# One read of 4608 bytes a row for q and k, and one for v, from the third pair of heads on

## The chip, the cores and the metric

The kernel runs on one core of one Trainium2 chip. The metric is device time in microseconds (us) of one launch. Before the change three runs took 440.33, 440.87 and 443.41 us; the median is 440.87. One more execution was taken with the profiler on: it took 437.04 us, of which 435.3 us lie between the first and the last profiled instruction (the span).

## The reference

Inputs are q, k and v of 8 batches, 8 heads, 576 positions and 64 channels in fp32, a forget gate f, and three weights. Decay attention comes first, then a gated MLP with a causal convolution of five taps:

```python
scores = scale * np.matmul(q, k.transpose(0, 1, 3, 2))
cum = np.cumsum(np.log(np.clip(f, 0.0001, 1.0)), axis=-1)
decay = cum[:, :, :, None] - cum[:, :, None, :]
scores = np.where(causal, -1000000000.0, scores + decay)
attn = softmax(scores)                      # rows, with 1e-9 in the sum
x = np.matmul(attn, v)                      # heads side by side: 512 channels
gate_pre += conv_w[k] * xp[:, k:k + S, :]   # summed over 5 taps
out = (1 / (1 + np.exp(-gate_pre))) * (x @ w_val) @ w_out
```

## The kernel before

Heads are taken two at a time: one head on partitions 0 to 63, the other on 64 to 127. That gives 32 pairs, four to a batch. The letters below are used throughout.

- **Loads.** `load_pair(i)` reads q and k of pair i into one of three buffers `Xr` (128 rows of 1152 fp32): two reads of 576 elements (2304 bytes) a row, q and then k. `load_rest(i)` reads v of the pair into one of three buffers `vt`: a read of 640 elements and one of 512.
- **S**, the scores (`plan_s`): small matmuls on 64x64 tiles give q times k plus the decay, in three groups of PSUM banks. VectorE (DVE) finds each row's maximum (line 421, written to `negm`), ScalarE (ACT) takes the exponential into `P` (line 425).
- **T and U** (`plan_pt`): DVE turns the 32x32 blocks of `P` into `T` (line 460), two copies fill half of `U` (line 250, on ACT, DVE or GpSimd, which is POOL in the rows), and four DMAs of `T` fill the other half from other partitions.
- **PV** (`plan_pv`): 108 matmuls on 64x64 tiles of `U` with `vt`, then three DVE steps (line 517) that multiply by the row sums' inverses (`zb`, which goes through DRAM as `zd`) and give `x`. Of `x`, `xh` and `xl` are the high and the low part.
- **Mv and Mo** (`plan_moe`): per batch the two products with the weights, each as three matmuls of high and low parts on the full 128x128 array. They are the bulk of TensorE's (PE's) work from the first batch on.
- **Start.** The gate f is clipped, its logarithm is summed (scan), and `split` cuts the sums into three bf16 parts that are placed in `st_70`: three casts with two DVE steps between them (line 347). The S matmuls of pair 1 and later read `st_70`. Both weights are decoded by DVE, ACT and POOL beside the first pairs (lines 693 to 709, tiles `sl`, `sh`, `ot`, `wall`), and pairs 0 and 1 take the convolution on PE (**CV**).

No scheduler runs: the string `ORDER` holds, packed, one list of all steps in the order of issue, the engine of each step that has a choice, and the PSUM bank of each product. Every engine, and the queue of SP that starts nearly all DMAs, works through its part of that list in order. A DMA on SP waits for the one eight places ahead of it to land, besides the semaphores of its data. Lines 235, 250 and 262 are helpers that record matmuls, copies and DMAs, so these rows are told apart by their tiles.

Of the kernel before, what the change touches and what calls it, by code (L numbers as in the profile page):

```python
# [41 lines left out]
NF = 16  # L42
PART = ((0, 32, 48), (0, 16, 32))
ORDER = (
    "c-l>pc}!G!w#Vz<y0!0n)vf*3erw<N?beRI1kjfN`bSgpk_Pz$kVzDsL`o-7WD=mA1ZZB;(EcIlB!G4T=p+s8OB&=Qio8USKN@rrK_>y^4?$k?prmKstyKNaId#tGd(Q"
# [3 lines left out]
    "4h=EQAQbLy(Xo;3DxEagA_|{s!nEbP-AfkQ^jaz)fJ3be-~o@{za;>;qTHT(FnWMH!<EQYtBvq&kWO9Hu-aE)!2v_-u%Tkq?P`L^^4L(n~3kU*Yhe21G$OxJ8+v)Kd!N"
    "CdvV2meNgL1uMWL*h*;v?-Qm76ND;omas|zs5_K(%3JUZnN3PjQ>4?(^W-$;A(_r@CO43W$nE4b^DeoAvOuW^TftxH{d9x`lTebAbQKgc&Vf{_gt|eWr0>!Z#t0o_R8U"  # L50
    "=vP5M54lnyeM=+pE$dXQ0Im>AWJ?+G8ld*riJ3S))NqlQUoyq4;r=1Jq^8qy9}MY2#i_!;sXd4YU~u}&_5Fn)=A0B(}i_-~k8#vAhglAD;dj1FcGbB5W+_(TRNt<2w;T"
    "g*=8EOUohPim${sOPEeR4R+Zx=b~)8>nlXF6IGqf!Rf+QOtNA<qinoC6t#;fHlY*W76;?Y9AG2PcR3l!^|@*7aL|3*dx@>)Jj@C<35{B3(#EnpQvHHhO)$-W3Mu6XkuC"
    ";euX_sE#QOfBCU>v&=Rz6dPIPuH8X}7cj?y{^Xwt~GN&5<ka3gI&Zxz=;b*8d><jo=>J|JXyN%t)o@NiQe`Zi=MRqm&3cHc5;@-e_;lIN_WvE%_nfDlv8B2^3`z*78Wn"
    "wKbDrg(*Vf<xUT0j>;qIT94EzP>kZf1E{5!N-<Y1VbxbLuJs<!*Cc(8ll+`2V5)Ok2Rerma%{PJM!ZiJ!$EaO${JF2EgOzrk<dx2Qd|ewvBG;hJb$_?xVc92vWw>*O}l"
    "D!5f#7cImcp>@&L8A<LfRts0lJ}sb2cBq4_OSBPIA8VAh&)8vX&=zPN+%9g7pqJap{lJ!T5Y8vIh4Wf)$mVk(37zwf198%vqF|6qVGeUQX%Wt8&Li3f#wQxgZ4``gHv}"
    "HeXIg+Rrh~#J?prRN`GmD8pa@4<w*+m1E$*CPkBg&I>63z8!H7UbPtd2i6WnF)6~Vs1MDG*GnQL5?h)-YSKI8J32=l*K3oMlBW=;zR1eKh5!KmPr@D=L~3*w=oN)cbg="
# [36 lines left out]


# [698 lines left out]
```

## Time and profile before

| quantity | value |
|---|---|
| median of three runs | 440.87 us |
| profiled execution | 437.04 us, span 435.3 us |
| PE matmul busy | 416.7 us (96%) |
| DVE busy | 373.7 us (86%) |
| ACT busy | 338.1 us (78%) |
| POOL busy | 287.9 us (66%) |
| DMA traffic of the SP queue | 85.28 MB in 74328 packets, 71.1% of 16 engines |

Busy shares are means over stages that differ. The reader should look at which engine is full in which stage, and what TensorE waits for where it is not full. Idle time of an engine that nothing waits for costs nothing.

### The profile page before, as it was taken

The numbers are of one execution on the slowest core, as the hardware profiler recorded it, in microseconds if no ns is written. First come the engines' busy times: TensorE is split into PE (matmuls) and PEld (weight loads), VectorE is DVE, ScalarE is ACT, GpSimd is POOL, SyncE is SP. The second block draws the span as 40 slices with busy tenths as digits, with TensorE's granted clock in tenths as the row PEclk, the third lists the DMA queues.
The fourth block names the chain that finished last, engine by engine and source line by source line (L and its number), as shares of the span: only waits on it lengthen the run. The fifth ranks groups of instructions, "written<-read, shape, count | busy, mean of one in ns | idle before, by whom it ended". The sixth has DMA issues, their size and how long they took to land.

```text
span 435.3 us, 16742 instructions
## 1 busy us (share of the span) xinstructions
PE 416.7 (96%) x6660; PEld 356.1 (82%) x6660; DVE 373.7 (86%) x1034; ACT 338.1 (78%) x840; POOL 287.9 (66%) x295
## 2 busy tenths in 40 slices
PE   7679899999999989999999999999999999999996
PEld 5456678888998878888898889887898888988885
DVE  6999889998999888898899987978999987997751
ACT  7899879998888869888777877667987988763430
POOL 4575847587959692898779475898675779752200
PEclk9899999999999999999999999999999999999999
DMA  7889987878777975977885677777867776387112
GB/s 286 291 213 240 239 233 196 223 206 210 216 202 199 253 199 152 256 211 200 220 249 143 184 212 206 197 209 216 243 174 209 223 184 191 74 205 224 57 46 98
DMA packets 74694, 86.93 MB, mean 200 GB/s; under 512 B 48120, under 2 KB 48120, under 8 KB 74616
## 3 DMA queue, kind: packets, MB, share of 16 engines
q1 hardware_dynamic: 74328, 85.28, 71.1%
q8 instruction: 52, 0.85, 0.8%
q10 hardware_dynamic: 288, 0.59, 0.4%
q14 instruction: 26, 0.21, 0.2%
HBM read 51.99 MB, written 10.26 MB: 143 GB/s over the span
## 4 chain that ended last, share of the span: by engine, by line
PE 88%; DVE 4%; DMA 3%; ACT 2%; issue 1%; POOL 1%; SPq 0%; POOLq 0%
PE banks L235 88%; DVE banks L421 2%; DMA U<-T 1%; DMA vt<-in_v_dram 1%; DVE T L460 1%; ACT P L425 1%; DMA cwu<-in_conv_w_dram 1%; POOL wall L709 1%; DVE negm L421 0%; ACT L334 0%; SPq L262 0%; POOL U L250 0%; DVE sh L707 0%; ACT sl L693 0%; ACT gate L333 0%
## 5 line engine op out<-in xcount | busy, mean ns | idle before, releaser
L425 ACT ACTIVATE P<-banks,negm 128x576 f32<-128x576 f32 (+8 forms) x288 | 150.0, 530 | 42.4 <-DVE negm L421 30.7
L421 DVE CUSTOM_DVE_ANT_0 banks<-banks,mk 128x576 f32<-128x576 f32 (+8 forms) x288 | 135.3, 508 | 15.2 <-PE banks L235 11.4
L562 POOL TENSOR_TENSOR gate<-gate,tm 128x576 f32<-128x576 f32 x77 | 109.7, 1425 | 33.6 <-DVE gate L560 12.0
L460 DVE STREAM_TRANSPOSE T<-P 128x1088 f32<-128x1088 f32 (+2 forms) x96 | 110.5, 1165 | 5.2 <-ACT P L425 2.8
L235 PE MATMUL banks<-xh,wall 128*128 128x288 f32 x512 | 107.1, 298 | 0.0
L235 PE MATMUL banks<-Xr 64*64 64x288 f32 (+8 forms) x1280 | 103.1, 410 | 1.4 <-DMA Xr<-in_x_dram 1.4
L235 PEld LDWEIGHTS banks<-U,vt 64*64 64x64 f32 x3456 | 91.8, 135 | 8.3 <-issue 3.1
L235 PE MATMUL banks<-U,vt 64*64 64x128 f32 (+1 forms) x3456 | 93.2, 256 | 3.8 <-issue 1.8
L235 PE MATMUL banks<-wall,hh 128*128 128x512 f32 x288 | 90.4, 395 | 0.0
L235 PEld LDWEIGHTS banks<-xh,wall 128*128 128x128 f32 x512 | 83.3, 188 | 4.2 <-issue 1.4
L235 PEld LDWEIGHTS banks<-Xr 64*64 64x64 f32 x1280 | 63.8, 134 | 16.5 <-issue 5.9
L235 PE MATMUL banks<-xl,wall 128*128 128x288 f32 x256 | 75.4, 295 | 0.0
L235 PEld LDWEIGHTS banks<-wall,hh 128*128 128x128 f32 x288 | 52.6, 188 | 13.0 <-issue 1.6
L425 ACT ACTIVATION_READ_ACCUMULATOR P<-banks,negm 128x1 f32 x288 | 58.7, 204 | 0.0
L250 ACT COPY U<-T 128x1440 f32<-128x1440 f32 x40 | 55.5, 1396 | 3.4 <-DVE T L460 1.7
L235 PE MATMUL banks<-wall,hl 128*128 128x512 f32 x144 | 56.2, 390 | 0.0
L235 PE MATMUL banks<-st,pk 64*64 64x448 bf16 (+8 forms) x620 | 45.8, 291 | 7.5 <-ACT st L250 3.7
L257 POOL TENSOR_SCALAR tm<-x,cw 128x576 f32<-128x576 f32 x40 | 30.1, 753 | 34.1 <-DVE gate L560 13.3
L235 PEld LDWEIGHTS banks<-xl,wall 128*128 128x128 f32 x256 | 48.0, 188 | 0.3
L607 POOL TENSOR_TENSOR hl<-h,hh 128x576 fp32r<-128x576 f32 (+2 forms) x34 | 34.4, 1027 | 12.6 <-DVE gate L560 4.1
L526 POOL TENSOR_TENSOR xl<-x,xh 128x576 fp32r<-128x576 f32 x25 | 35.6, 1430 | 10.6 <-DVE sl L695 4.9
L235 PEld LDWEIGHTS <-pk 64*64 64x64 bf16 x620 | 25.6, 106 | 20.0 <-issue 16.2
(104 smaller groups left out, 482.8 us busy)
## 6 DMA issues: line engine op xcount, KB each, us to landing
U<-T SPq DMA_DIRECT2D x128, 180.0 KB
Xr<-in_x_dram SPq DMA_DIRECT2D x63, 288.0 KB
vt<-in_v_dram SPq DMA_DIRECT2D x32, 320.0 KB
out_dram<-ot SPq DMA_DIRECT2D x36, 256.0 KB
vt<-in_v_dram SPq DMA_DIRECT2D x32, 256.0 KB
zb<-zd SPq DMA_DIRECT2D x64, 80.0 KB
zb<-zd SPq DMA_DIRECT2D x64, 64.0 KB
sl<-in_w_out_dram SPq DMA_DIRECT2D x2, 512.0 KB
```

What stands on the lines that cost most here:

```text
L235: nc.tensor.matmul(out, lhsT=lhsT, rhs=rhs, start=start, stop=stop)
L250: (eng.copy if eng is nc.scalar else eng.tensor_copy)(out=out, in_=in_)
L257: eng.tensor_scalar(out=out, in0=in_, scalar1=col, scalar2=0.0, op0=ALU.mult, op1=ALU.add)
L421: nc.vector.tensor_tensor_reduce(out=sl, in0=sl, in1=mk[:, S - ext:], op0=ALU.add, op1=ALU.min, scale=-0.125, scalar=3.0e38, accum_out=neg ...
L425: nc.scalar.activation(out=dst, in_=bank(key)[:, a0:a0 + ext], func=AF.Exp, bias=negm[r][:, col], scale=-1.0, accum_out=zs[r][:, col])
L460: nc.vector.transpose(out=bass.AP(Tt.tensor, Tt.offset + 32 * FB[js[0]], [pitch, (32, nk), (CW, 2), (1, 32)]), in_=Pt[u])
L526: any_("xl", {"POOL": 1.4, "DVE": 0.67}, p, lambda eng: eng.tensor_tensor(out=xl[s], in0=xv, in1=xh[s][:, :].bitcast(F32), op=ALU.subtract ...
L562: eng.tensor_tensor(out=gt, in0=gt, in1=to, op=ALU.add)
L607: eng.tensor_tensor(out=hl[jj][:, y:y + x1 - x0], in0=h2[jj % 2][:, x0:x1], in1=hh[jj][:, y:y + x1 - x0].bitcast(F32), op=ALU.subtract)
L709: any_(nm, {"POOL": 1.2, "DVE": DM / 960.0 + 0.075}, p, lambda eng, lo=lo, zz=zz, m=m: eng.tensor_tensor(out=lo, in0=zz, in1=m, op=ALU.mul ...
```

## The change

From pair 2 on `load_pair` issues one DMA for the whole row of q and k (1152 elements, 4608 bytes) and `load_rest` one for the whole row of v. Pairs 0 and 1 keep two reads each. Consumers are the same: S of a pair waited for both halves of `Xr` before, and PV for both parts of `vt`. The list in `ORDER` is another one, for all engines.

```diff
 ORDER = (
-    "c-l>pc}G!G!w#Vz<y0!0n)vf*3erw<N?beRI1kjfN`bSgpk_Pz$kVzDsL`o-7WD=mA1ZZB;(EcIlB!G4T=p+s8OB&=Qio8USKN@rrK_>y^4?$k?prmKstyKNaId#tGd(Q"
+    "c-l>pdrTC2mdCrQtKaYHclEpaUHyJ{SHG(t2(k$ve*n74h3g-JYy#*cf^Kp_C%JH$1dvI9>n4J3BIqW7P6Ay2xS*3<kWCPsM9@tx=p=$nBFH9!OtR4So!RPi|IRsm&gX"
...
     def load_pair(i):
         r = i % XB
+        if i > 1:
+            load("load", 1.62, i - 1.0, Xr[r], x[i], (), [("Xr", r, n) for n in range(2)])
+            return
         for n in range(2):
             c = slice(S * n, S * n + S)
             load("load", 0.81, i - (1.0 if i else 9.0) + 0.02 * n, Xr[r][:, c], x[i][:, c], (), [("Xr", r, n)], early=i == 0)
 
     def load_rest(i):
         r = i % 3
+        if i > 1:
+            load("load", 1.5, i - 0.2, vt[r], v[i], (), [("vt", r, n) for n in range(2)])
+            return
         for n, c in enumerate((slice(0, 5), slice(5, NJ))):
             load("load", 0.75, i - (0.2 if i else 7.0) + 0.02 * n, vt[r][:, c], v[i][:, c], (), [("vt", r, n)])
```

Sixty DMAs go: 30 of `Xr` and 30 of `vt`. SP starts 406 instead of 465, since one read of pair 0 that ACT started is now also started by SP. Line numbers of the changed kernel are 5 higher behind the loads and 1 lower ahead of them.

The order of VectorE near the start, from the first of the two steps that cut the summed logarithms (`gate` is their buffer, `st_70` the bf16 table) to the first turns of pair 0. Before:

```order
L347 SCALAR_TENSOR_TENSOR gate<-st_70,sel,gate 128x576
L421 ISA banks,negm_90<-banks,mk 128x64
L421 ISA negm_90 128x1
L250 CAST st_70<-gate 128x576
L421 ISA banks,negm_90<-banks,mk 128x128
L421 ISA negm_90 128x1
L347 SCALAR_TENSOR_TENSOR gate<-st_70,sel,gate 128x576
L421 ISA banks,negm_90<-banks,mk 128x384
L421 ISA negm_90 128x1
L460 STREAM_TRANSPOSE T_83<-P_81 128x16x2x32
```

The same place on VectorE with the change:

```order
L352 SCALAR_TENSOR_TENSOR gate<-st_70,sel,gate 128x576
L426 ISA banks,negm_90<-banks,mk 128x256
L426 ISA negm_90 128x1
L426 ISA banks,negm_90<-banks,mk 128x128
L426 ISA negm_90 128x1
L706 TENSOR_SCALAR sh<-sh 128x512
L352 SCALAR_TENSOR_TENSOR gate<-st_70,sel,gate 128x576
L426 ISA banks,negm_90<-banks,mk 128x384
L426 ISA negm_90 128x1
L465 STREAM_TRANSPOSE T_83<-P_80 128x17x2x32
L465 STREAM_TRANSPOSE T_83<-P_81 128x16x2x32
```

The cast between the two steps is gone from VectorE; of the three casts before S of pair 1 two were VectorE's and one ScalarE's, now all three are ScalarE's.

The queue of SP around the four DMAs that fill `U` for pair 2 (`U_85<-T_83`, the second use of that buffer; `zd` and `zb` are the row sums on their way through DRAM, `ot` receives weights here). Before:

```order
L262 DMA zd_68<-zt_96 4x32x32
L262 DMA Xr_78<-in_x_dram 128x576
L262 DMA U_85<-T_83 32x1440
L262 DMA vt_87<-in_v_dram 128x640
L262 DMA zb_98<-zd_68 64x4x64
L262 DMA Xr_76<-in_x_dram 128x576
L262 DMA U_85<-T_83 32x1440 x2
L262 DMA zb_98<-zd_68 64x5x64
L262 DMA U_85<-T_83 32x1440
L262 DMA Xr_78<-in_x_dram 128x576
```

The same place on SP with the change:

```order
L261 DMA Xr_77<-in_x_dram 128x1152
L261 DMA zb_99<-zd_67 64x5x64
L261 DMA U_85<-T_83 32x1440
L261 DMA zb_99<-zd_67 64x4x64
L261 DMA zd_68<-zt_96 4x32x32
L261 DMA U_85<-T_83 32x1440 x3
L261 DMA zb_98<-zd_68 64x5x64 x2
L261 DMA zb_98<-zd_68 64x4x64
L261 DMA Xr_76<-in_x_dram 128x1152
L261 DMA zb_98<-zd_68 64x4x64
L261 DMA ot<-in_w_out_dram 128x1024
L261 DMA vt_87<-in_v_dram 128x1152
```

No read stands between the four any more: the read of `vt_87` (v of pair 3) and that of `Xr_76` (pair 6) now stand behind them, and a whole read of `Xr_77` (pair 4) ahead of them.

## Rows read from the trace of the kernel before

**Rows 1.** The page's first part: busy us, share of span, instructions.

```profile
span 435.3 us, 16742 instructions
PE 416.7 (96%) x6660; PEld 356.1 (82%) x6660; DVE 373.7 (86%) x1034; ACT 338.1 (78%) x840; POOL 287.9 (66%) x295
```

**Rows 2.** Busy time by stage: PE, PEld, DVE, ACT, POOL, clock, DMA share, GB/s.

```profile
0.00:11.00 11.00, 8.23 (x95) 6.52 (x96) 6.96 (x21) 8.02 (x13) 5.23 (x29) 1.00 0.80 285
11.00:44.00 33.00, 25.44 (x446) 19.08 (x448) 32.55 (x101) 31.31 (x88) 20.92 (x25) 0.95 0.85 247
44.00:62.00 18.00, 16.00 (x236) 11.96 (x228) 14.64 (x44) 14.30 (x36) 12.12 (x11) 0.91 0.95 246
62.00:396.00 334.00, 332.05 (x5511) 287.47 (x5512) 297.59 (x829) 274.70 (x689) 246.05 (x228) 1.00 0.75 203
396.00:435.30 39.30, 34.95 (x382) 31.12 (x380) 22.00 (x42) 9.74 (x18) 3.62 (x3) 0.99 0.28 90
```

**Rows 3.** Chain of work that ended last, in order of time: start, us, what.

```profile
46.37 5.02 DMA U<-T
62.15 95.26 PE banks L235 x1351
```

**Rows 4.** Timeline of PE, start of the kernel: start, us, group, [idle before].

```profile
1.41 2.82 PE L352 MATMUL banks<-ident 128*128 128x128 f32 x12 [1.41 <-POOL ident L285]
5.59 2.00 PE L235 MATMUL banks<-Xr 64*64 64x288 f32 x26 [1.36 <-DMA Xr<-in_x_dram]
...
15.46 0.64 PE L235 MATMUL banks<-st,pk 64*64 64x448 bf16 x8 [3.65 <-ACT st L250]
```

**Rows 5.** Groups by form, of DVE and then ACT: busy us, mean ns.

```profile
L460 DVE STREAM_TRANSPOSE T<-P 128x1088 f32<-128x1088 f32 x32 | 41.6, 1300 | 2.7 <-DMA U<-T 1.1 <-DMA vt<-in_v_dram 0.9 <-ACT P L425 0.6
L250 DVE CAST st<-gate 128x576 bf16<-128x576 f32 x2 | 1.0, 488 | 0.0
...
L250 ACT COPY U<-T 128x1440 f32<-128x1440 f32 x40 | 55.5, 1396 | 3.4 <-DVE T L460 1.7 <-issue 1.1 <-PE banks L235 0.4
L250 ACT CAST st<-gate 128x576 bf16<-128x576 f32 x1 | 0.7, 668 | 0.0
```

**Rows 6.** Timeline of PE around PV of pairs 1 and 2.

```profile
40.71 2.70 PE L235 MATMUL banks<-U,vt 64*64 64x128 f32 x105
...
49.96 0.43 PE L235 MATMUL banks<-U,vt 64*64 64x128 f32 x4 [0.55 <-ACT P L425]
51.52 4.34 PE L235 MATMUL banks<-U,vt 64*64 64x128 f32 x104 [1.12 <-DMA U<-T]
```

**Rows 7.** Busy time by stage again, around PV of pair 2.

```profile
50.00:55.00 5.00, 3.88 (x97) 3.67 (x101) 3.19 (x6) 3.94 (x15) 3.47 (x4) 0.75 0.98 238
52.50:55.90 3.40, 3.40 (x78) 3.28 (x68) 1.28 (x2) 1.92 (x5) 0.97 (x2) 0.51 1.01 241
```

**Rows 8.** The page's DMA queues (packets, MB, share) and DMA issues.

```profile
q1 hardware_dynamic: 74328, 85.28, 71.1%
...
q10 hardware_dynamic: 288, 0.59, 0.4%
...
U<-T SPq DMA_DIRECT2D x128, 180.0 KB
Xr<-in_x_dram SPq DMA_DIRECT2D x63, 288.0 KB
```

**Rows 9.** Timeline of SP: one read of half a pair's q and k.

```profile
47.30 0.58 SPq L262 DMA_DIRECT2D Xr<-in_x_dram  x1
```

**Rows 10.** Timeline of PE: first matmuls of Mv behind an S.

```profile
66.19 0.40 PE L235 MATMUL banks<-xh,wall 128*128 128x288 f32 x1
66.42 0.29 PE L235 MATMUL banks<-xl,wall 128*128 128x288 f32 x1
66.55 0.42 PE L235 MATMUL banks<-xh,wall 128*128 128x288 f32 x2
```

**Rows 11.** The last pair: busy time by stage, timeline of ACT, timeline of PE.

```profile
374.00:396.00 22.00, 22.00 (x251) 20.00 (x250) 18.90 (x41) 15.49 (x32) 12.43 (x10) 1.00 0.69 184
...
392.27 2.71 ACT L250 COPY U<-T 128x1440 f32<-128x1440 f32 x2 [1.09 <-issue]
...
403.70 1.67 PE L235 MATMUL banks<-U,vt 64*64 64x128 f32 x63 [0.78 <-issue]
```

More of the change, by code (lines that the diff above doesn't have):

```diff
@@ L49 @@
[L49 to L56, printed above, removed]
@@ new lines @@
+    "4Jf{rlB#Y6tF^aC<3%XuSqW{wUh>+fpP|@gzBM2pcCo^nrWA5?<hy)H<a6?M#?y}0C}NBXcp>$WYkMQ2XGx=Q7%y5Q@m7^`VLryrhsuULbXx}Dokmkg46-(Jz76dN}UB"
+    "6)GF#8WtiGUou+NlYN-d5c4{|u5p19?&|Z+<LQhDqp*xg^pppVncAz<69{5bVLK^}0p(ALO)<uJ<FTmH-G3qEVK%1q3^i3*EU!<+ko&ooPRp2$?rx+Lpik;F;8>ep3Vw"
+    "4sNO8<r-r!(l23@d$@wgvQ1x+o8+9h4464`YwU0AX+s5OJFrZpKAA&KRS~K|Oc?v@$vwWY9~;z;*B*rJpfHNi!n!9qKYQ20o_xzzltcvQLF*PpL1deA+qo5p|t0!q{Mp"
+    "GRhcj^m$4p;{tn*QBG&muF=oa)8GVSo>2xiff?Eo1EFCwlvc;61p6t~^mFujuoZmH7-FBIwXwGu9$GuQm;Ro;%I;z>uy4?B(U*CH^dBi#!5#2`VP~+Jd+cuZ8XM%m964"
@@ new lines @@
+    "u<eHPR+--4eQQQ83eHvND-&Sr2H*>m)1`UHKRz6(~;Fs7ebL(_7n*&-&yoMo@kU(iub7kCIF<iF8z?pe-lE<kSJEO9Yz1-Fjd#GT_#aNp85*&W;-u9BH$rnv(0b8bD&!"
+    "_|?00Kd?m(QV`@?mYJuuZ+7#Z{=pm&72ssnpw~7<o0vRnKuMA%r<5dvw^wC+vKftt(<n|M<$C*W(axb*<DO8`GDtU)$pU_80Q-2GRMPdBr_P@Od+F--@tF<xAPnMrQ~k"
+    "@E2fMUX8p?i%+#_F-UydqRdceO8=P`ZFXxZUDsnA(i`PaTVg8BvExDb1oeZ+JnOocqu7P)ptmM8CWqBZfo?OGC^I^W1-^b}8-(lV)6Z~&jKMPPk#v0>{a3(l%ekuPxGs"
+    "3s>kGKrhD7jBCz_;^aylugfV4ut8LA(j_9CL|0BA6oonfaXj6M2#~#ClC06-)@K_=kcS)@{}%d0j9iXklGp4NCmHm%MHA5))>XvKBc@{9S>Z0l?1%8-nM|F4igD8P*+s"
@@ new lines @@
+    "6RVEb&6?*_@fvswEIvHJdM{dJ;cyzhAV%Ol(JCK<=LEz2n=B99Cf32PST9&NWT5yns|-F6{mNp9nebKK3(jlKb+`wf;%u?n#a-e7aV0Eclh}Xbyyd*%?{VfhS~i2-Egl"
+    "v><v->>;2-fH@nz!cyf2&|cw}y`pcaP3gxD)a#iimZaYS4zwu)~{_F04QWq61Gjz1xplI-(Ig4g0X$u+ncJ`b-*8pKQiEI<Tz;al*bgelz=KZ3`^58y_gmHo5qKY0x93"
+    "_LH<2>_`;dXx7f?-K7%Jgqd$9v4sWwk31C1$Y(q2qJ=aq8L&pU4oZnyOK)jj(80gu`jD^g42R^$-3-NhDmYhl-MKPkYogB1ZM@`3g&rf=}l>$Ff6<xOtC+}pWrX>CY%x"
+    "u2`hx(36~^@v`)G$n-SIs*^(piOYw8rh_sAdChQT82_K7>#ZSezB>UnG8DG9D1LR_1gAkWv@_K2b^rGOBfFkUZjmQu=Q#c_@%SUD7!bahgj4wfiIyojmB)=dYxn5`!dW"
@@ new lines @@
+    "4W<6+tEKg0y50*+k0ZO!)zFS6a>9LinOy*=OO3@Mob+L=wFcUJ@<|=VT9sOwp!r4XKrE2_H$HN^eLXNUupBOHt7k<h10BWDJ=`tfFzmBe^a=g)|_SrM=QdWES~FI;pBc"
+    "29PeK79puOrK{3!CBsNJ(j#A&+BJSQsPKutQ+*QRimQ@~l1q{=QcTTMw;`2skNTZ9i(FF;%4_A#^7HZ@)dEr@x-J<}EvYWcAISSvVbM1tKsKtHQ(cp9t9DfkMU!Y<MJQ"
+    "M@p+YDtSInyf>IoI19ulQQS46i(mqkj&ccKkdspz?COR7^JsuVJhY+Mx9L?xHhdKs=JG`Hji#f+v|v8h?rENDtKHd$0wEvi;*X%;nAnhtf3s8+M4nUQ~z-jzR+FUkFi1"
+    "^KG{liaR2rzn@5SKLthH5W8pngLC<?1Q{i-K_p19~3<jwdl0ELG>-PS3Rt0(~N1><UP6$U72n~x2I`QbSb(u<C=C&MlC=(b^W>?MTf$seJj7C=vPc@>U5ayl(IoHs_T~"
@@ new lines @@
+    "2%Bt0O)#ugqx*rwi)NbXB=%eC5(;#b-waGeU6vU&WE15`IR;dHDM&z@CudGmpl|PHTT2P7W(z->F0;y9XN(}j^olp?Un3k=bRUB#o9aAUJJybkVyh87(4cdC82Lbg>x@"
+    "q-<Zc$;;>y!&>SYM^TrQSm~Q9^%C`@OP7xu#&~<@#EEwf3!UTQ{e^sPyU&&{BOwzi&izHsuS&Tg5NRKIIkVh_XvLr~9OSt)5h_C`DSO_JR2>I-}e|r*wZ+-$S<)qso0<"
+    "R@<PTMrYBNx^nFs-M0FR8qgf+UW%4=>&pAe1?2*|h<>B}&eWl8(>7_{CXz{nKGi|!dFzf=Y2&LVOsIYp-B2#7r%e4?mga-9$5dykH(k>Is26H3>R+f8nvY7E>a!9zm6;"
+    "F|(^P5dH?dKjNnlEw#`GhmCX-GzYHBsjm_Ze0dT(AZubMlxi{=UKnt53J$s|L=7PqQGHD^LC9i}P^VX<2F%%J6g{)Qe!y=brgn%=G&)IZW6nqbSkDXgkd)mj)9xuw){U"
@@ new lines @@
+    "~aJdpuMC0N&8UyMEgwpLfdHBG<z)=+G6doKGr|gFY6(5y=u`ELHn&8)=uk+zRki`y)#uiKUz!CZ&5<EuD@@|pl8stsKKl>i_ANwLo0y2G2ONz*rtBYx~<n?yLu+JWL>v"
+    "TSf?#t^lbA>(~*&ExQO-{Dh%%p_Y4;dLx$g>ofZK$Zym8>7~B2W^3w8qv;*xyr>tw*4XaM`+}eP(TW(qITAEems;8Dg%eHmJ&|>H?j2T`TY77mANkbE+GJG_!3_?Sv0W"
+    "+Y6IfKRAYq^Z|qdkUA!@MD4@EI}&4~Clw^P$0Fdt+&~-m`gaUh}kV)%MH~u>r;!8_Q@h@{Mj|siDiZW|J8gY>T!E<0JEcjj*-ZN^K3cr=DwA7HhQ4+S+ZnvC8(16EzaX"
+    "VOzHiu}85|bF2BZ@vOPt+~I6;ZrXlzE?c&psQp*VMe~^LgYBxB>8i%IEv?Q@XP<Mzd1(2)dDnL6tTDD2=bR(XC1;<}V7r0Y?d8}xtll_?H5*5rQ_knkd8feDW8Sj>)*k"
@@ new lines @@
+    "1&bJuyr$g*}C0T<#r;}TfUm{ryx<B(hCUT}{Z$J}f?>bAPa-G4MMy1j1HI)p{65x2-r@*dfGv6%gw({G3DBj!=_w0i=pbK%}oZkx5&$n-uimfO#}vi2@_l^gMnVLI2Wy"
+    "Tb0XW~>eFY3yIDRn|ItgWckIZ*Oxq*=Mm@cdNbI-R}MicFpH^@g0-KzhciYo2%JHxYw~-YooivzKyXw18$vH;O(?iY%500yJCNWWnCio4cBGYE2G=-(f-OlW0X1m7h83"
+    "2xHpVxFYY+R*4-6erft(cV(+$lybH!<Pq{1R+HqfVt$1$Q@7RB`AGu)<<WYL+yr`qYyY4x(Z+pIXr5*L&4bOf1L;Dl^_r6Z=uBXX6<{EL$_zpb-t{Xms2XF{%t=@6hJx"
+    "8Bo(ox}9w9mTAysN%F-+*t}*W=yv4LM#0W1eN>zWais-#hQBakMy|cv+6qjycDgZ^=968~4%u4UPrhm}AlR!u6xK!*Sqy=6dbohaPyne$)^97aVuJe$SR~!)5nG{JXAB"
@@ new lines @@
+    "ht)6lV<FIA7Q#a*Po3wbcgOqA`^fv)yJP$&ROLZJ&m3i*eeVa?RsRo;tDY~e6$jzJ<hkzY2sMRzLesu3{~7;Bhc4s^r9+jW-ta3&XQ)5a8mbFzIJ!Nb9e}gmQ|f={`ZY"
+    "Kb+72EDcY{Fav-g+qQ233P=>vVR&+TM}_QKQQu`n3v^$+?l``ONB|6Tu%<Cfp*llx}F<6*w@rsqe`9nXu<dg!9(zdWnq&2Yds?ZJI|AK=dT&iGFI&ica6bN=)GccHEDT"
+    "9^?z2*VMXQx=)@dn0Ish%AIhLv#Kmf7)q{L?T)If&VD_DD*T`fiL*$@Kt{kzJecxbk6b6<Ir-bG&1Y?A@U~pec)8U9q=c2Lalg9pdR1G*Ztf6sz|->5U&W-1=jKUNNwa"
+    "wpexW92nRawk-%I31`b4t06hlB1|r|#qk&yq9-G4_@DUu1(Zk=zpm1|!KXfB<(f7sw$<GLo1HwQ#ek;<0Go$6s%Moj=J}`<;;r;kLj)vjzKui&^JM{r1-0F*j!?EdDL#"
@@ L92 @@
+    "jF(^pU*GlWhLw+T2fIGE~zQ$E72wG$#h9eiM^!0WT>RMq`YLb<Uz@mlFpLe5{Lwl$RzOiLn1-P7L`Ohwt(Z`6Yu1q9LK<8pL`sl9Dh%q6Z<4eIsTs5Uu#YxC-t;rn^d5"
+    "Zj{OrR={QC$_&~v;9G_6}JjsI!K2*#<p#TM)6Gd8qeo_e(^=ZfFZ#|F-1gOCHN~07!YT=|6$fSZYSm@*=11S7+(hpGVA1ZWDE9n0=J6NDojxAb&PAk+?3VBeG1{K-BKh"
+    "#JC>epVVMH*O)f88MYADf~4gG?>@<l;PEE1+V8R)_$_9H`g_t)TyPtN)ywRM^eeX{ZI8TDT>saK})Q0~F{`@n)f7_18(iPC_ZF(h7SA3nWUhQ%Zpd{=ZxQYX7z)a<Oly"
+    "xFMjR`p<WVT8x0j*l!bk-5s^qJyggA3Jgl|Z6p`xp%(RiBhw1E1r{=BMJ+Pv{{YNBr*8"
 )
```

48 lines of the change are left out of this document (9 added, 39 removed).

## Prediction

> **What bounds the kernel now.** I read the page first, then busy time by stage, then the chain of waits with the timeline of TensorE where it stands still. TensorE is busy 416.7 of 435.3 us [rows 1], but stages differ. From 62 to 396 us it is busy 332.05 of 334 us at a clock of 1.00 [rows 2], and the chain of waits runs along it [rows 3]: in that stage only fewer or cheaper matmuls count, and every other engine has room (VectorE 297.59 of 334). Before 62 us TensorE is busy 8.23 + 25.44 + 16.00 = 49.67 us, so it stands still for 12.3; behind 396 us for 4.35 [rows 2]. The reader should see who is full in the first stage: VectorE, 32.55 of 33 us from 11 to 44 us, with ScalarE close behind at 31.31. From 44 to 62 us nothing computes without pause and the DMA engines are the fullest, at 0.95 [rows 2]. So the change can earn at most the 12.3 us of the start, what the clock loses there, and a little at the end; and it can lose anywhere that a new wait reaches TensorE.
>
> **The reads themselves.** Sixty DMAs go, thirty of q and k and thirty of v. SP needs 0.58 us to start one [rows 9], 60 x 0.58 = 35 us of its queue. I cost that at nothing: SP's time lies beside TensorE's, and TensorE waits for a DMA only at the first read [rows 4] and once for `U` [rows 6]. If that cover were gone, a `U` behind a read would start up to 0.58 us earlier. On the DMA engines 60 x 128 = 7680 row packets become part of longer ones; the bytes stay. Price bounds: nothing, if time goes by bytes; and if it went by packets alone, the small queue q10 gives it: 0.4% of 16 x 435.3 us over 288 packets, 97 ns, nearly all of them rows of 2304 bytes [rows 8], so 7680 x 97 / 16 = 46 us of all engines' time. q10 moves 0.59 MB in 288 packets, q1 85.28 MB in 74328 [rows 8]: 97 against 67 ns for 2049 against 1147 bytes, so more bytes take more time, and I take the low end, nearer nothing. The Trainium skill's page DMA: Bandwidth & Descriptors (Specifications) speaks against any gain here: it asks 512 bytes for line rate, which the old rows of 2304 bytes already had; by it the longer row would be worth zero, by the packet bound up to 46 us of engine time. On the path the choice matters little: wherever DMA time shrinks, TensorE can get back no more than the one `U` wait of 1.12 us.
>
> **VectorE at the start.** Up to x of pair 0 VectorE's list holds the same instructions as before less two casts into `st_70`, and so does it up to the last turn of pair 2. Two casts at 488 ns are 0.98 us [rows 5], on the engine that is 99% busy there. ScalarE takes them at 668 ns each, 1.34 us, and gives up one copy of `U` of 1.396 us to GpSimd [rows 5]; its balance is zero. Effect: **-1.0 us** on everything that VectorE's chain releases up to 44 us. Bounds: -1.0, and +0.6 if the last cast, which now queues on ScalarE behind exponentials and a weight step, reaches S of pair 1 later than the 15.46 us of before [rows 4] by most of its own length. I take -1.0, because VectorE has two turns of pair 0 (1.3 us for one of them, rows 5) to do before it needs S of pair 1. Eight of the warm-up matmuls move in front of the first S: 12 take 2.82 us [rows 4], 8 take 1.88, and 1.41 + 2.82 + 1.88 = 6.1 us is 0.5 us behind the old start of S at 5.59 [rows 4]. The read of pair 0 that moved from ScalarE's queue to SP lands in that time too. VectorE's steps for the logarithms and weights cover this; without the cover it costs 0.5 us.
>
> **`U` of pair 2.** PV of pair 2 begins at 49.96 us and stands for 1.12 us on a DMA of `U` [rows 6], which took 5.02 us to land [rows 3] with the DMA engines at 0.98 [rows 7]. In the new queue the read of `Xr_76` and that of `vt_87` stand behind these DMAs. Counted from the first instruction, half a read of `Xr` (288 KB) and both reads of one `vt` (576 KB) that stood ahead of them stand behind them: 864 KB, at the 246 GB/s of that stage [rows 2] 3.6 us of transfer. So the wait should go: **-1.1 us**. Bounds: -1.1, and +1.2, if the merged read of `Xr_77` just ahead of them, 288 KB more in one piece (1.2 us at 246 GB/s), is what they queue behind. I take the first, since the sum ahead is smaller. What is late next is v of pair 3, whose PV comes some 10 us later.
>
> **TensorE's own list.** The matmuls are the same. Changes between 64x64 and 128x128 tiles go from 66 to 62; two of these four are warm-up pieces in the waiting stage. The first matmul behind a change takes 0.23 us to the next, later ones 0.13 [rows 10], so a change costs 0.1 and the other two are worth **-0.2 us**; bounds 0 and -0.4.
>
> **The end.** Both copies of the last `U` ran on ScalarE, 2.71 us [rows 11]; now one of them is GpSimd's, so it is ready some 1.3 us sooner. Against that six matmuls of Mv (0.8 us) that stood before the last two PV stand behind them. TensorE stood for 0.78 us inside the last PV, released by nothing in the profile [rows 11]. I take zero; bounds -0.8 and +0.8.
>
> **Sum.** -1.0 - 1.1 - 0.2 = -2.3 us: the profiled execution of 437.04 us would become 434.7. That execution lies 3.8 us below the median of 440.87, and I carry the difference over: 440.87 - 2.3 = **438.6 us**.
>
> **Rival one: the clock holds as well.** In PV of pair 2 the granted clock is 0.51 from 52.5 to 55.9 us, the lower of its two levels, behind 0.55 and 1.12 us of idling in a thin stretch [rows 6, 7]. That PV takes 4.34 us against 2.70 for pair 1's [rows 6]: 1.6 us. If the waits there go, the fall may go with them, and the 0.55 us wait for an exponential goes with the earlier VectorE; with another 0.4 us of the small waits that VectorE's head start removes: -2.3 - 1.6 - 0.55 - 0.4 = -4.9, 436.0 us. The Trainium skill's page TensorE: Matmul & The Clock Gate (HAM oscillation) says that waits for DMAs between bursts of matmuls make the clock fall; the rows agree, and by that rule the fall would go with the wait. Against it: the thin stretch before stays thin, since VectorE bounds it.
>
> **Rival two: nothing arrives.** The casts on ScalarE cost what VectorE gains, and `U` of pair 2 queues behind the merged read as it did behind two halves: 440.9 us. ScalarE at 31.31 of 33 us speaks for it.
>
> **Rival three: slower, merged reads in front of `U`.** A whole read puts 288 KB more in one piece before any `U` that follows it on SP, 1.2 us at 246 GB/s. Where `U` lands with less than that to spare, TensorE waits, in the stage where it never waits now; what VectorE does before the last turn also grows by several us against 3.1 us of idling [rows 11]. The point that decides is four such pairs: 4 x 1.2 = 4.8 us, 445.7 us. For it: DMA at 0.75 in the full stage [rows 2]. Against it: no pair after the third waits for `U` now, so some reserve is there.
>
> **Numbers.** Differences under 1% (4.4 us) can't be told from none. Chances: forecast 0.38, rival one 0.33, rival two 0.14, rival three 0.15. Rival one alone ends more than 1% faster, rival three alone more than 1% slower: faster 0.33, within 1% 0.52, slower 0.15. The forecast's own range is 436.5 (with half the clock's loss returned) to 442.5 (with `U` later and the cast late: +1.2 + 0.6). The range of 8 in 10 adds rival one down to 434 (with two more us of waits at the start) and leaves out rival three: 434 to 443 us.
>
> **What would show it.** Right: TensorE is full some 1 to 2 us before 62 us; x of pair 0 comes about 1 us before its old time; no wait for `U` at PV of pair 2; from there to the end TensorE's busy time is as before within 1 us. Rival one shows as a clock of 1.00 through PV of pair 2. The forecast is wrong if TensorE waits for `U`, `vt` or `Xr` between 62 and 396 us, or if S of pair 1 begins later and the first stage ends later with it.

## The result, and the profile after

The change made the kernel a little slower: 442.32 us against 439.50 (medians of 22 runs each; the three runs ahead of the prediction lay somewhat high). The ratio is 1.0076, with a 95% interval of 1.0055 to 1.0097; it is taken over the runs in the chip's faster state alone, so it is not just the quotient of the two medians, 1.0064. That lies inside the range of 434 to 443 us, but the forecast was 0.5% faster. The profiled execution took 442.47 us, 5.4 more than that of before.

The first part of the page of the changed kernel, to be held against [rows 1]:

```profile
span 440.7 us, 16679 instructions
PE 415.6 (94%) x6660; PEld 357.3 (81%) x6660; DVE 375.3 (85%) x1036; ACT 334.8 (76%) x835; POOL 288.4 (65%) x297
```

TensorE computes no longer than before (415.6 against 416.7 us); the time is in waits. The stages show where. The columns are those of [rows 2]:

```profile
0.00:11.00 11.00, 9.21 (x100) 7.37 (x100) 6.47 (x21) 7.33 (x11) 4.35 (x32) 1.00 0.77 268
11.00:44.00 33.00, 22.16 (x334) 16.56 (x337) 29.20 (x88) 28.31 (x81) 19.98 (x22) 0.90 0.80 233
44.00:62.00 18.00, 16.64 (x344) 13.16 (x337) 17.38 (x56) 16.89 (x47) 14.27 (x14) 1.00 0.76 202
62.00:396.00 334.00, 326.80 (x5483) 284.11 (x5483) 298.90 (x833) 269.11 (x677) 242.95 (x226) 1.00 0.76 205
396.00:441.00 45.00, 40.79 (x411) 36.15 (x409) 23.32 (x43) 13.16 (x23) 6.82 (x7) 1.00 0.30 93
```

The full stage, 62 to 396 us, was busy for 332.05 us [rows 2] and is now busy for 326.80. From 11 to 44 us TensorE does 3.3 us less and VectorE, which was full there, stands still for 3.8. From 44 to 62 us there is somewhat more work (16.64 against 16.00), at a clock of 1.00 where 0.91 stood; in the first 11 us there is more too (9.21 against 8.23), most of it the warm-up matmuls that moved there. The timeline of TensorE names the stops (start, us, group, idle time before and what ended it):

```profile
16.95 0.64 PE L234 MATMUL banks<-st,pk 64*64 64x448 bf16 x8 [4.93 <-ACT st L249]
...
52.20 2.71 PE L234 MATMUL banks<-U,vt 64*64 64x128 f32 x108
...
62.05 0.70 PE L234 MATMUL banks<-st,pk 64*64 64x288 bf16 x6 [1.18 <-ACT P L430]
...
69.18 0.35 PE L234 MATMUL banks<-st,pk 64*64 64x384 bf16 x4 [1.03 <-DVE x L522]
...
84.03 0.22 PE L234 MATMUL banks<-st,pk 64*64 64x64 bf16 x2 [2.61 <-issue]
...
145.09 0.32 PE L234 MATMUL banks<-st,pk 64*64 64x320 bf16 x3 [1.59 <-issue]
```

S of pair 1 begins at 16.95 us instead of 15.46 [rows 4]. PV of pair 2 runs in one piece, without the wait for `U` and at full clock (2.71 us against 4.34, rows 6). The new stops follow behind it. Set side by side, the start of the last matmul of each PV, after minus before:

| PV of pair | 0 | 1 | 2 | 3 | 4 | 5 | 10 | 11 | 28 | 31 |
|---|---|---|---|---|---|---|---|---|---|---|
| us later | +2.6 | +2.7 | -0.9 | +1.2 | +2.4 | +4.4 | +6.8 | +5.3 | +5.9 | +4.3 |

So 2.7 us are lost at the start, 3.6 are won at pair 2, and some 8 are lost up to pair 10; behind pair 11 little moves until the last three pairs give 1.6 back. Behind the last PV 1.1 us are lost once more, so that the span ends 5.4 us later.

### The profile page after: what moved, and what is told of

Same layout as the page of the kernel before. It is cut to its first block, busy times and chain, and to the rows that moved or that the text cites. A ratio compares the mean times of both kernels' runs of the same rounds, so it can differ in the third digit from the quotient of the medians.

```text
span 440.7 us, 16679 instructions
## 1 busy us (share of the span) xinstructions
PE 415.6 (94%) x6660; PEld 357.3 (81%) x6660; DVE 375.3 (85%) x1036; ACT 334.8 (76%) x835; POOL 288.4 (65%) x297
## 3 DMA queue, kind: packets, MB, share of 16 engines
q1 hardware_dynamic: 65832, 85.57, 70.3%
## 4 chain that ended last, share of the span: by engine, by line
PE 73%; DVE 9%; DMA 8%; SPq 3%; issue 3%; ACT 2%; POOL 2%; DVEq 0%; POOLq 0%
PE banks L234 73%; DVE banks L426 3%; SPq L261 3%; DVE T L465 2%; DMA U<-T 2%; DMA zb<-zd 2%; DVE x L522 1%; DMA Xr<-in_x_dram 1%; DMA sl<-in_w_out_dram 1%; DMA lnf<-gate 1%; POOL U L249 1%; POOL wall L714 1%; DVE negm L426 0%; ACT P L430 0%; DVE gate L565 0%
## 5 line engine op out<-in xcount | busy, mean ns | idle before, releaser
L430 ACT ACTIVATE P<-banks,negm 128x448 f32<-128x448 f32 (+8 forms) x288 | 149.3, 527 | 40.3 <-DVE negm L426 32.1
L426 DVE CUSTOM_DVE_ANT_0 banks<-banks,mk 128x320 f32<-128x320 f32 (+8 forms) x288 | 135.7, 506 | 18.2 <-PE banks L234 15.7
L567 POOL TENSOR_TENSOR gate<-gate,tm 128x576 f32<-128x576 f32 x76 | 107.9, 1421 | 21.0 <-DVE tm L256 6.9
L234 PEld LDWEIGHTS banks<-U,vt 64*64 64x64 f32 x3456 | 90.1, 134 | 8.0 <-issue 2.1
L234 PE MATMUL banks<-U,vt 64*64 64x128 f32 (+1 forms) x3456 | 91.1, 253 | 3.6 <-ACT P L430 1.6
L249 ACT COPY U<-T 128x1440 f32<-128x1440 f32 x43 | 59.7, 1396 | 3.9 <-issue 2.4
L234 PE MATMUL banks<-st,pk 64*64 64x288 bf16 (+8 forms) x620 | 46.4, 293 | 13.2 <-ACT st L249 4.9
L612 POOL TENSOR_TENSOR hl<-h,hh 128x576 fp32r<-128x576 f32 (+2 forms) x37 | 37.2, 1025 | 18.0 <-ACT hh L249 12.3
L234 PEld LDWEIGHTS <-pk 64*64 64x64 bf16 x620 | 27.4, 107 | 25.9 <-issue 22.3
L256 POOL TENSOR_SCALAR tm<-x,cw 128x576 f32<-128x576 f32 x42 | 31.8, 761 | 20.6 <-DVE gate L565 9.6
```

What stands on the lines that cost most here:

```text
L234: nc.tensor.matmul(out, lhsT=lhsT, rhs=rhs, start=start, stop=stop)
L249: (eng.copy if eng is nc.scalar else eng.tensor_copy)(out=out, in_=in_)
L256: eng.tensor_scalar(out=out, in0=in_, scalar1=col, scalar2=0.0, op0=ALU.mult, op1=ALU.add)
L426: nc.vector.tensor_tensor_reduce(out=sl, in0=sl, in1=mk[:, S - ext:], op0=ALU.add, op1=ALU.min, scale=-0.125, scalar=3.0e38, accum_out=neg ...
L430: nc.scalar.activation(out=dst, in_=bank(key)[:, a0:a0 + ext], func=AF.Exp, bias=negm[r][:, col], scale=-1.0, accum_out=zs[r][:, col])
L567: eng.tensor_tensor(out=gt, in0=gt, in1=to, op=ALU.add)
```

## The experiments

All ratios are to the kernel before. Two executions of one kernel can lie several us apart (the two traces with halves took 441.37 and 436.66 us), so a single trace shows where waits stand and the ratio shows what a kernel costs. "List" is the order of the steps; "whole" is one DMA a read. Every edit of the table concerns the reads from pair 2 on; with short rows, v of the first two pairs is read in other pieces too.

| kernel | list | DMAs a read | ratio | 95% interval |
|---|---|---|---|---|
| the changed kernel | new | 1 | 1.0076 | 1.0055 to 1.0097 |
| the same, again | new | 1 | 1.0051 | 1.0009 to 1.0094 |
| one DMA, short rows | new | 1 | 1.0084 | 1.0046 to 1.0122 |
| two halves | new | 2 | 0.9982 | 0.9946 to 1.0017 |
| two halves, again | new | 2 | 0.9991 | 0.9957 to 1.0026 |
| 1088 elements, then 64 | new | 2 | 0.9996 | 0.9957 to 1.0034 |
| three thirds | new | 3 | 0.9996 | 0.9964 to 1.0029 |
| only v in halves | new | 1 and 2 | 1.0040 | 1.0007 to 1.0074 |
| 64 elements, then 1088 | new | 2 | 1.0089 | 1.0054 to 1.0124 |
| the same, again | new | 2 | 1.0076 | 1.0038 to 1.0114 |
| whole, place of the first half | old | 1 | 1.0222 | 1.0168 to 1.0275 |
| whole, place of the second half | old | 1 | 1.0275 | 1.0216 to 1.0335 |
| halves, place of the first | old | 2 | 1.0291 | 1.0250 to 1.0333 |

**The reads or the list?** Four kernels: the new list with halves, the old list with whole reads, the new list without most reads of v, and the changed kernel again.

```diff
 # two halves (v likewise)
-load("load", 1.62, i - 1.0, Xr[r], x[i], ...)
+for c in (slice(0, S), slice(S, 2 * S)):
+    nc.sync.dma_start(out=Xr[r][:, c], in_=x[i][:, c])
```

> The changed kernel with each read from pair 2 on cut into its two halves again, started one right behind the other; the list is the new one. Theory A (the whole reads make the line that TensorE's own instruction fetches and the DMAs of U stand in): the stretches of 'issue' idling of TensorE at 81 us (2.61 us) and 143 us (1.59 us) shrink to 1 us or less in all, and the ratio to the kernel before falls from 1.0076 to 1.000 +- 0.003. Theory B (the list costs it): the ratio stays at 1.005 to 1.010, S of pair 1 still begins at about 17 us, and waits of the same sum stand between 60 and 160 us. Both: S of pair 1 at about 17 us, since the reads of pairs 0 and 1 are unchanged.

It gave 0.9982. Undoing the merge alone, with every byte at its place in the queue of SP, wins back the loss: the time is as theory A had it. S of pair 1 began at 17.61 us, so that loss belongs to the list, as both theories said. Waits of TensorE behind 62 us (what ended them, us in total, times, longest), in the changed kernel:

```profile
PE banks L234 <- issue: 4.8, 4, 2.6
PE banks L234 <- ACT P L430: 1.2, 1, 1.2
PE banks L234 <- DVE x L522: 1.0, 1, 1.0
PE banks L234 <- DVE zt L443: 0.7, 1, 0.7
PE banks L234 <- DMA U<-T: 0.4, 1, 0.4
```

and with halves, from the trace of the second measurement, whose edit is the same:

```profile
PE banks L234 <- issue: 1.8, 1, 1.8
PE banks L234 <- ACT P L436: 1.3, 1, 1.3
```

8.1 us against 3.1. The first measurement's trace has 6.1 us (2.1 of "issue", 1.6 for `x`, 1.4 for `P`, 1.0 for `U`), with a time of 441.37 us that is high for it. "Issue" did not go down to the 1 us of theory A: the stop at 81 us is still there, with 1.8 us in both traces of this kernel, so the merge alone does not make it.

> The changed list with two halves a read, once more, as the partner of the next kernel on the same chip: ratio 0.998 +- 0.003 by theory L; near 1.005 if the first measurement was chance.

0.9991: it held.

```diff
 # whole reads, old list
-c = slice(S * n, S * n + S)
+c = slice(S * n, S * n + S) if i < 2 else slice(0, 2 * S)
+if i > 1 and n:
+    ...   # the second half's step issues nothing
```

> The kernel before with whole reads from pair 2 on, each at the place of its first half; the second half's place is empty and all other steps stand as before. Theory A: slower than before by 2 to 4 us (ratio 1.005 to 1.009), with over 3 us of 'issue' idling of TensorE after 62 us where before had 2.8, and U of pair 2 later than before. Theory B: ratio 1.000 +- 0.003.

1.0222, nearly 10 us and more than theory A had. Waits of TensorE in this kernel, the whole span:

```profile
PE banks L235 <- DMA U<-T: 6.1, 7, 1.9
PE banks L235 <- ACT P L431: 4.3, 7, 1.3
PE banks L235 <- issue: 4.1, 6, 1.5
```

Before there was one wait for `U`, of 1.12 us [rows 6]; here there are seven. This is the picture of the prediction's third rival, found in the old list.

```diff
 # new list without the reads of v from pair 3 on
+if i > 2:
+    ...   # the step issues nothing
```

> The changed kernel without the reads of v from pair 3 on (29 x 576 KB of DMA left out; PV then uses old v). If TensorE's 'issue' stops are fetches of its instructions that wait behind data DMAs (A), the stops at 81 and 143 us go (under 0.5 us in all) and the time falls by 3 us or more against the changed kernel, ratio to before 1.000 or less. If the stops come from the rate at which TensorE uses up instructions (C), they stay at 4 us in all and the time falls by under 1 us.

0.9984 (0.9948 to 1.0020): 17.1 MB less gain as much as cutting the reads in two, and no more. The "issue" stops behind 62 us were 2.2 us, 1.40 of them at 84 us. That is neither A's figure nor C's, and hardly less than the 2.3 us that the next run has with all its reads.

> The changed kernel itself, once more, for a second trace. A and B: ratio 1.0076 +- 0.003; the 'issue' stops of TensorE stand at 81 and 143 us again, within 1 us of their length, and S of pair 1 begins at 17 us. If the stops are chance of one execution (D), they stand elsewhere or are gone, while the median ratio stays.

1.0051. The stop at 84 us was there again, with 1.20 us, that at 145 us was not, and "issue" behind 62 us came to 2.3 us in place of 4.8. So the one at 145 us came with one execution (D for that one). The one at 84 us stands in both traces of the changed kernel, but it hangs neither on the list nor on the merge alone: the new list with short rows has no stop of 0.7 us or more there, and the old list with whole reads has one of 1.46 us that ends at 82.23.

**The row or the number of DMAs?**

```diff
 # one DMA, short rows: gaps in the buffers
-XQ, XK = 0, S
+GAP = 16
+XQ, XK = 0, S + GAP
-Xr = tiles(XB, [P, XW], F32, "Xr")
+Xr = tiles(XB, [P, 2, S + GAP], F32, "Xr")
 # and vt as [P, 3, 6 * D + GAP]
```

> The changed kernel with one DMA a read as it has, but with gaps of 64 bytes between the pieces of a row in Xr and vt, so that the DMA's rows are short again: 2304 bytes for q and k, 1536 for v (the first two pairs' v is read in pieces of 768 and 384 elements). Theory L (the number of DMAs counts: a DMA on SP waits for the one eight places ahead of it, and with one DMA a read eight places hold more bytes; in the changed kernel U of pair 7 waited 2.0 us for a read of v that way): time as the changed kernel, ratio 1.005 to 1.008. Theory R (the length of the row counts: what shares a DMA engine with rows of 4608 bytes waits longer for its turn): as with two halves, ratio 0.998 +- 0.003.

```diff
 # two DMAs, long rows (v likewise)
+for c in (slice(0, XW - 64), slice(XW - 64, XW)):
+    nc.sync.dma_start(out=Xr[r][:, c], in_=x[i][:, c])
```

> The changed kernel with each read from pair 2 on cut in two DMAs, one right behind the other, of 1088 and 64 elements a row: rows of 4352 and 256 bytes. Theory L (number of DMAs on SP): as with two halves, ratio 0.998 +- 0.003, without SP waits of 2 us for a read of v. Theory R (length of the row): as the changed kernel, 1.005 to 1.008.

1.0084 and 0.9996, the intervals apart. Between these two the length of the row plays no part that shows, and the number of DMAs goes with the time. The page's queue row (packets, MB, share of 16 engines) of the changed kernel, then of the kernel with one DMA and short rows:

```profile
q1 hardware_dynamic: 65832, 85.57, 70.3%
```

```profile
q1 hardware_dynamic: 77608, 85.57, 71.9%
```

The rows were really cut: 11776 more packets. And the engines' time hardly depends on it: before it was 71.1% of 435.3 us [rows 8], 309.5 us; in the changed kernel 70.3% of 440.7, 309.8 us, with 8496 packets fewer. With short rows it was 318.2 us, but traces scatter as far without more packets: at 74472 packets each, the kernel with the small DMA first has 319.8 and 315.3 us and the one with halves 309.9 and 306.2.

**How the places matter.** Only v in halves, the other way round, and thirds:

> The changed kernel with v read in two halves from pair 2 on, q and k still in one DMA. If the reads of v alone hold up the queue (they stand between U and the row sums' DMAs), the ratio is 0.998 +- 0.003; if both reads count alike, it is about 1.002; if q and k alone do it, it stays at 1.005 to 1.008.

1.0040 (1.0007 to 1.0074): between the values for v alone and for q and k alone, as if both kinds of read counted, but the interval reaches nearly to each of them.

> The changed kernel with each read from pair 2 on in three DMAs of 384 elements a row. Theory L: three places a read hold SP back more, so waits of SP for reads grow and the row sums' and U's DMAs land as early as with two or earlier: ratio 0.994 to 1.000. If two were the best point and SP's own time counts (60 more DMAs at 0.58 us than two halves, 35 us of its queue), U starts later and the ratio is 1.001 to 1.006.

0.9996: no better than two; 60 more DMAs on SP than with halves cost nothing that shows either.

```diff
 # small one first
-for c in (slice(0, XW - 64), slice(XW - 64, XW)):
+for c in (slice(XW - 64, XW), slice(0, XW - 64)):
```

> As two DMAs with long rows, but the small one (64 elements a row) is started first and the one of 1088 right behind it, so nothing stands between the large DMA and what follows it on SP. Theory L (the eight places: a read that takes two of them lets SP run less far ahead): ratio as with the large one first, 0.9996 +- 0.003. Theory S (the 0.58 us that SP spends on a second DMA behind the large one is what helps, by spacing): back to the changed kernel, 1.005 to 1.008.

1.0089: theory L in the form stated (places alone) fell, since the number of DMAs is the same as in the kernel that gave 0.9996. SP's waits for earlier reads, which L took for the cause, do not bear it out either: for `Xr` and `vt` they sum to 4.6 us in the changed kernel and to 11.5 with 1088 elements first, the faster of the two. Theory S had it. Since the gap was surprising it was measured again:

> The small DMA of 64 elements a row first and the one of 1088 behind it, once more. If the order of the two counts, 1.005 to 1.012 as before (1.0089); if its first measurement was chance and only the number of DMAs counts, 0.996 to 1.003.

1.0076: the order of the two counts. To tell S from other reasons, the small DMA was then started one step of SP later:

> Two DMAs a read again, 1088 elements a row and then 64, but the small one stands one step later on SP, behind the step that followed the read. Theory S (the DMA next behind the large one suffers unless 0.58 us of SP lie between): as the changed kernel, ratio 1.005 to 1.009. Theory L (the eight places: with two places a read the DMA that waits for the large one to land stands one step nearer, whatever lies right behind it): as with the small one right behind, 0.9996 +- 0.003.

1.0225, but this figure says nothing about S and L. Some small pieces stood behind the S or PV that reads them (which so used old data). One then waited for TensorE and held the queue of SP; its row (what was waited for, us, times, longest):

```profile
SPq L279 <- PE banks L234: 8.0, 1, 8.0
```

A `U` behind it made TensorE stand for 5.09 us, the longest stop for a DMA in any of these traces. Without such pieces:

> Two DMAs a read, 1088 elements a row and then 64 one step later on SP, but never behind the S or the PV that reads the buffer (in the kernel before this one two kinds of pieces stood there, and one held SP for 8.0 us, so its 1.0225 answers nothing). Theory S (0.58 us of SP must lie between the large DMA and what follows it): as the changed kernel, ratio 1.005 to 1.009. Theory L (places): as with the small one right behind, 0.9996 +- 0.003.

1.0031 (0.9996 to 1.0065): between the two figures, inconclusive. Last, whole reads that let one DMA pass:

```diff
 # each whole read one step later on SP (v likewise)
-load("load", 1.62, i - 1.0, Xr[r], x[i], ...)
+put_off(("Xr", i), lambda: nc.sync.dma_start(out=Xr[r], in_=x[i]))
```

> The changed kernel with whole reads, each one step later on SP: the DMA that stood right behind a read (mostly zb, zd or U) now stands ahead of it. Theory H (what stands right behind a whole read is late by the read's bytes, and that is the cost): ratio 0.997 to 1.003. If the cost lies with the number of places or with SP's lead in general, it stays at 1.005 to 1.009. If reads one step later come too late for S and PV, TensorE waits for Xr or vt and the ratio is over 1.009.

1.0286 (1.0227 to 1.0344). H's figure did not come, and the idea that a read may move by a step at no cost fell. Where SP's longest waits lay, in the changed kernel and then in this one:

```profile
SPq L261 <- DVE negm L426: 28.1, 15, 3.9
```

```profile
SPq L261 <- DVE negm L442: 39.8, 15, 11.2
```

A read that stands behind a step that waits is late by that wait, and so is all that stands behind it on SP. TensorE itself waited 0.7 us for `Xr` and 9.8 for `P`, probably for S whose steps came late. The test of H is thus clouded: the reads themselves came late, and whether what follows a whole read is late by it stays open.

**The old list's places.** Both halves at the first's place, and the whole read at the second's:

> The kernel before with both halves of each read from pair 2 on started together, at the place of the first. It differs from the kernel before in where the second half stands, and from the kernel before with whole reads in the number of DMAs alone. If the number of DMAs is what costs 2.2% there, ratio 1.000 to 1.008; if it is that the second half's bytes stand earlier, in front of U, ratio 1.015 to 1.025.

> The kernel before with whole reads from pair 2 on, each at the place of its second half (the first half's place is empty). Theory E (in the old list whole reads cost 2.2% because the second half's bytes stand earlier, ahead of U and the row sums): ratio 0.997 to 1.006. Theory N (one DMA a read costs it wherever it stands): 1.015 or more. If the first half now comes too late for S and PV, TensorE waits for Xr or vt, which the waits would show.

1.0291 and 1.0275. Theory E and theory N each have one of them against it: in the old list two DMAs at one place cost as much as one DMA at either place. Its two halves stand apart, and any other arrangement that was tried costs 10 to 13 us.

**The casts.** The list's loss at the start was tried by itself: the third cast into `st_70` moved from ScalarE to VectorE, at its place in the list.

```diff
+casts = [n for n, nd in enumerate(self.nodes) if nd["cls"] == "cast"]
 for w in steps:
+    eng = "DVE" if w >> 3 == casts[2] else codes[w & 7]
```

> The changed kernel with two halves a read, and the third cast into st_70 on VectorE at its place in the list. In the changed kernel this cast waited 0.94 us on ScalarE behind a weight step and an exponential, and S of pair 1 began at 16.95 us, 1.5 us later than before. If the path to S of pair 1 is the chain of the casts (C), S of pair 1 begins 0.8 to 1.1 us earlier than with two halves alone, and the ratio falls by 0.1 to 0.3% from 0.998. If it is VectorE's sum of work (V, as predicted), S begins earlier but PV of pair 1 is as late as with two halves alone or 0.4 us later, and the ratio stays.

> Two halves a read and the third cast into st_70 on VectorE, once more beside its partner: 0.2 to 0.3% below it and 0.3 to 0.6% below the kernel before (C); equal to its partner within 0.1% if VectorE's sum is what counts (V).

S of pair 1 in the trace with halves alone, then with the cast moved:

```profile
17.61 0.64 PE L234 MATMUL banks<-st,pk 64*64 64x448 bf16 x8 [5.11 <-ACT st L249]
```

```profile
16.75 0.41 PE L236 MATMUL banks<-st,pk 64*64 64x448 bf16 x8 [3.75 <-DVE st L251]
```

0.86 us earlier, as C had it; PV of pair 1 came 0.4 us earlier. In the second pair of traces S came 0.9 us earlier and PV of pair 1 0.2 us later, which is V's picture. The time doesn't settle it either: 0.9952 (0.9915 to 0.9989), then 1.0042 (0.9997 to 1.0087), with its partner at 0.9991. No version that surely beats the kernel before was found.

## Why the prediction was wrong

**The reads themselves: the step that failed.** "I cost that at nothing", because SP's time lies beside TensorE's and TensorE waits for a DMA only twice. The bytes were argued rightly: for the same bytes the DMA engines took 309.5 and 309.8 us, and the long row was worth nothing that shows. What failed is the cover. The runs put the merge at 1.0076 and 1.0051 against 0.9982 and 0.9991 in the same list, 2.6 to 4.1 us. The step counted the 60 DMAs as work and asked what hides it; it never asked what the one DMA in place of two does to what follows it on the same queue. A stage without waits at 0.75 of DMA use [rows 2] was read as one with reserve.

Where the loss lies can be said in part. The last matmul of PV of pair 2 starts at 54.7, 56.0 and 56.0 us in the three traces with one DMA a read (the changed kernel twice, short rows), and at 54.4, 54.5 and 54.8 in three with two (halves twice, 1088 and 64): 1.0 us on average. Behind 62 us TensorE's waits sum to 8.1, 6.8 and 7.1 us against 6.1, 3.1 and 6.2: 2.2 us. Together that is 3.2 us, as much as the ratios say. It is spread over waits for `x`, `P`, `U` and "issue", and which of them is long differs from trace to trace. The two traces with the small DMA first do not fit this: PV of pair 2 at 55.6 and 54.6 us and waits of 5.7 and 5.8 us, though the kernel costs as much as the changed one (these two executions were 1.9 and 2.8 us below their medians). So the place of the loss is not shown.

What an "issue" stop is, the one that ended at 84.03 us shows. DMA queues from 81.40 to 82.60 us (packets, MB, share of the 16 engines):

```profile
q1 hardware_dynamic: 345, 0.43, 101.0%
q8 instruction: 1, 0.02, 5.0%
```

The queue of instructions moves one packet here, just after TensorE stopped at 81.41 us, while the engines are full of data; TensorE goes on at 84.03. In the 4.9 us ahead of it no such packet moved, and data took 91.9% of the engines. The stop that ended at 145.09 us is much the same, with its one packet between 142.6 and 143.7 us, begun before TensorE stopped at 143.50. In both TensorE went on 1.5 us after the packet's end. All traces together have 23 "issue" stops of over 0.7 us behind 62 us, and in 22 of them TensorE went on 1.2 to 1.7 us after the end of such a packet. There are 52 such packets on the page, for 2 x 6660 matmuls and weight loads: 256 each. The Trainium skill's page Runtime: NRT & Kernel Launch (Instruction fetch mechanics) says that instructions come in blocks of 256 over a DMA queue of their own, and that this is mostly hidden. The count agrees; here it wasn't hidden for up to 2.61 us. So these stops are in all likelihood fetches of instructions that came late. That they are late because they wait behind data is not shown: in the 3 us ahead of each of the 22 packets the DMA engines were busy for anything from 65% to all of the time, and the run without most reads of v had 2.2 us of "issue" left, against 2.3 in the second trace of the changed kernel.

**Why two DMAs help is not settled.** Shown: the length of the row doesn't explain the time (1.0084 with short rows), the bytes ahead of `U` don't explain it (they are the same with halves), and a small DMA behind the large one helps where the same one ahead of it doesn't. The Trainium skill's page DMA: Bandwidth & Descriptors (Queues, rings and completion order) says that a DMA engine takes a whole packet of descriptors from one queue before it turns to another; if a packet were one DMA's share, a fetch would wait for half as long behind half a read. The short rows and the halves agree with that. The kernel with 1088 elements first doesn't: its large DMA is nearly a whole read, and yet it gave 0.9996. So the rule is not shown to be the cause. That SP's 0.58 us behind the large DMA do it (S) fits both orders, and the run with the small DMA one step later neither bears it out nor excludes it. Which mechanism makes one DMA dearer than two stays open.

**VectorE at the start (-1.0): wrong.** The list did free VectorE, but VectorE's sum wasn't the path: from 11 to 44 us VectorE, which had waited 0.2 us for matmuls before, now waits 3.2 us for them:

```profile
DVE banks L426 <- PE banks L234: 3.2, 3, 2.1
```

S of pair 1 waits for the chain of subtractions and casts. The last subtraction, in the timeline of VectorE in the changed kernel:

```profile
14.55 0.81 DVE L352 SCALAR_TENSOR_TENSOR gate<-st,sel,gate 128x576 f32<-128x576 bf16 x1
```

and what ScalarE did until the cast that needs it:

```profile
15.08 0.76 ACT L708 ACTIVATE sh<-sh,ebias 128x512 int32<-128x512 int32 x1
15.72 0.52 ACT L430 ACTIVATE P<-banks,negm 128x320 f32<-128x320 f32 x1
16.13 0.20 ACT L430 ACTIVATION_READ_ACCUMULATOR P<-banks,negm 128x1 f32 x1
16.22 0.67 ACT L249 CAST st<-gate 128x576 bf16<-128x576 f32 x1
```

The cast's data was ready at 15.36 us; it began at 16.22, behind a weight step and an exponential. That is the case of the upper bound that was named (+0.6) and not taken; S of pair 1 came out at +1.5, beyond that bound. A later S of pair 1 is also one of the signs of being wrong that the prediction gave. PV of pair 1 was 2.7 us late. Not all of that is the cast's: with the cast on VectorE again S gained 0.9 us and PV of pair 1 gained 0.4 in one pair of traces and lost 0.2 in the other. What else holds PV of pair 1 is not shown. The cover for the eight warm-up matmuls held: the first S began at 5.51 us, not later than the 5.59 of before.

**`U` of pair 2 (-1.1) and the first rival's clock: right, and given back.** The wait went, and with it the low clock in that PV. But S of pair 1 ran in a low stretch before as well, 3.4 us long like the one at pair 2, and that one now lasts twice as long. Before, from 14.9 to 18.4 us:

```profile
14.90:18.40 3.50, 2.94 (x38) 2.51 (x41) 3.25 (x11) 3.17 (x10) 3.49 (x4) 0.51 0.94 304
```

After, the stages 14.9 to 21.7 and 52.0 to 55.0 us:

```profile
14.90:21.70 6.80, 4.75 (x56) 4.02 (x59) 5.85 (x15) 5.66 (x19) 4.57 (x6) 0.52 0.91 330
52.00:55.00 3.00, 3.00 (x117) 2.85 (x110) 2.97 (x13) 2.83 (x9) 2.84 (x4) 1.00 0.92 300
```

6.8 us at half clock in one piece, where two pieces of 3.4 lay before, one here and one at pair 2 [rows 7]: the clock's loss only moved. So the 3.6 us that pair 2 won stand against 2.7 lost in front of it, and PV of pair 2 is only 0.9 us early.

**TensorE's own list (-0.2)** is below what the runs resolve. **The end (0)**: the stop of 0.78 us in the last PV [rows 11] is gone, and the last three pairs won 1.6 us, but 1.1 us are lost behind the last PV, where the six matmuls of Mv now stand. That leaves -0.5, inside the bounds of -0.8 and +0.8.

**The list as a whole** was forecast at -2.3 us; with halves it gives 0.9982 and 0.9991, some 0.4 to 0.8 us, with intervals that hold zero. **Rival three** (0.15) had the sign and, at 4.8 us, nearly the size; its mechanism, more bytes in front of `U`, shows in the old list with the whole read at the first half's place (seven waits for `U`, 6.1 us), but not with it at the second's (one wait, 0.9 us, at 1.0275), and not in the changed kernel, where waits for `U` behind 62 us were 0.4 us.

**The range.** Its lower end of 436.5 does not come out of the reason given: half of the 1.6 us of the clock is 0.8, which makes 437.8.

## What to carry to other kernels

A queue of transfers that an order was fitted to is not free to change where the compute engine has no idle time to show for it: try the merge with the list held fixed before a new list hides what it costs, and do not price a DMA by its bytes and its start alone. When a step starts is read from the chain that releases it (subtract, cast, subtract, cast), not from the busy sum of the fullest engine. And "issue" idling of TensorE in a full stage can be its own instructions arriving late.
